# Earlier projections, earlier mask and earlier weight loads in a chain of attention, gated experts and channel mix

## The chip, the cores and the metric

One Trainium2 chip, one core. The metric is the device time of one execution in microseconds. The kernel before took 582.27 us, the median of three runs (582.23 to 583.47).

## What is computed

Three layers in a chain, float32, for 4 batches of 8 heads, 512 local and 32 global positions, width 64 a head.

```
s_ll = where(|i - j| <= 32, scale * q_l k_l^T, -1e9)      # local rows: window of 32 on both sides
a_l  = softmax([scale * q_l k_g^T, s_ll]);  out_l = a_l @ [v_g, v_l]
out_g = softmax(scale * q_g [k_g, k_l]^T) @ [v_g, v_l]    # global rows: all keys
x = concat(out_g, out_l), heads side by side              # (4, 576, 512): 544 computed tokens, 512 wide

logits = x @ w_gate; the two best of 4 experts, softmax of their logits as w
for each expert e: a = softmax(causal(scale * (x wq[e]) (x wk[e])^T)); y_e = a (x wv[e]) wo[e]
x = sum over the two chosen experts of w_e * y_e

xk = mu_k * x + (1 - mu_k) * x_prev;  xr = mu_r * x + (1 - mu_r) * x_prev     # x_prev: the token before
out = sigmoid(xr @ w_r) * (relu(xk @ w_k)^2 @ w_v)
```

## The kernel before

**Local attention, steps 0 to 35.** A loop `for n in range(NU + 4)` with NU = 32 holds the first layer as a pipeline written out by hand: step n forms the scores of two heads and half the sequence (`a_qk`, tile S, 16 matmuls), adds the mask and takes the row minimum on VectorE (`band`, tile sm, mn), and takes the exponential on ScalarE. `a_norm(n-1)` divides by the sum (rc on VectorE, pn and glob on GpSimd), `a_tp(n-2)` transposes (pT on TensorE, copied to `pts` by ScalarE or VectorE in turn). Four steps make a unit u; once a unit come the scores of the global rows (`g_qk`, Sga, pg), their weighting (`g_norm`) and transposes (`g_tp`), and `a_pv`, the product with V (tiles x, xg), which is written to `xT[b]`. Two units are one batch, so batch 0 is complete after unit 1, in step 10 or so.

**Second layer.** `b_split(b, half)` rounds a half of batch b's tokens into a high part (VectorE, L343) and a low part (GpSimd, L344), tile x00 for batch 0, half 0, then x01, x10 and on. `b_groups(b)` makes fifteen closures a batch, the splits and the projections: `b_qk` (tiles pb00q0 and on, 12 matmuls each, results in tile qk) and `b_v` (pv00 and on). A product of two float32 values is three matmuls on high and low parts (lines 93, 94, 95). The projections of batch 0 are called in steps B0 = 26 to 33 of the loop; `c_step` then runs nine causal-attention units a batch (scores C, row minima csm, transposes cT, product y) from step CS = 34 on, with the projections of the next batch between them; `last_rows` and the units named `l` do the 32 last rows (Ll, Lg, and the gate gb, gl).

**Weights and constants.** `load_wb(step)` fetches the weights of Q, K or V (rawwq, rawwk, rawwv), and `split_wb(step, c)` rounds one of their four chunks with a ScalarE cast (L154) and a GpSimd subtraction (L155). The load stands at step WB + 4 step (4, 8, 12), and one chunk is rounded in each of the four steps from there. The mask `band` is the last of four DMAs that ScalarE's queue issues at the start. At step 10 the loop fetches constants, `mu` among them, and computes `omu = 1 - mu` on VectorE.

**What sets the order.** The program is written as above, and a scheduler puts each engine's instructions in order when the kernel is built; on the chip each engine then works through its list in that order. An instruction that waits holds up all that stand behind it on its engine. Tiles come from pools: tag "x" holds one tile, and raw weights and the split tokens share it, so rawwk waits for the last subtraction of wq, x00 for the last subtraction of wv, x01 for the last matmul that reads x00. PSUM tag "a" holds six banks, taken in turn by S, Sga, pT, xg and the projections. The SP queue issues its DMAs in order, and each waits for the DMA eight places before it.

**Third layer.** From about 400 us to the end the channel mix; nothing of it is in the change.

Of the kernel before, what the change touches and what calls it, by code (L numbers as in the profile page):

```python
# [28 lines left out]
NU_D = 256  # L29
MIX, K0, FIRST = 32, 33, 4  # L30
V0, VS = 31, 2
WB, WS = 4, 4
LPOS, LPOS0 = 3, 3
B0, CS = 26, 34
BIG = 3.0e38
EPS = 1e-9
SCALE = 0.125
# [8 lines left out]
def chain_kernel(ctx: ExitStack, tc: tile.TileContext, kq, vw, vgd, w_gate, wq, wk, wv, wo,  # L46
# [12 lines left out]
    def T(tag, shape, name, dt=F32, bufs=None):  # L59
        return sb.tile([128] + list(shape), dt, tag=tag, bufs=bufs or BUFS[tag], name=name)  # L60
# [107 lines left out]
    for i in range(2):  # L168
        nc.gpsimd.memset(ptg[i][:, 4, :], 0.0)

    def load_pair(P, parts=1):
        t = T("kp", [NQ], f"kq{P}")
        if parts == 1:
            nc.sync.dma_start(t, kq[P])
        else:
            for eng, a, b in ((nc.sync, KT0, KT0 + 480), (nc.scalar, 0, 256), (nc.sync, KT0 + 480, NQ),
                              (nc.scalar, 256, 512)):
                eng.dma_start(t[:, a:b], kq[P][:, a:b])
        kqs[P] = t

    def load_v(P):
        t = T(("raw", "y", "wo")[P // 2 % 3], [2 * NB, 2 * HD], f"vw{P}")
        nc.sync.dma_start(t, vw[P].rearrange("p (j c) -> p j c", c=2 * HD))
        vws[P] = t
# [51 lines left out]
    def a_tp(n):  # L236
        u, r = divmod(n, 4)
        if r == 0:
            pts[u] = T("qk", [4, 4, 128], f"pt{u}")
        t = pn.pop(n)  # L240
        pT = ps_t(f"pT{n}")
        for k in range(4):
            nc.tensor.transpose(pT[:, k * 128:(k + 1) * 128], t[:, k].rearrange("p a b -> p (a b)"), ident)  # L243
        dst = pts[u][:, r].rearrange("p a b -> p (a b)")
        if r % 2 == 0:
            nc.scalar.copy(dst, pT)
        else:
            nc.vector.tensor_copy(dst, pT)
# [50 lines left out]
    def a_pv(u):  # L299
        b, g = divmod(u, 2)  # L300
        pt, pgt, tg = pts.pop(u), ptg[u % 2], tgs.pop(u)
        gp = ps_t(f"xg{u}")
        xs = [ps_x(f"x{u}{pp}") for pp in range(2)]
        for pp in range(2):
            v = vws.pop(2 * u + pp)
            for blk in range(2 * NB):
                m, c = divmod(blk, 2)
                for h in range(2):
                    rr = slice(64 * h, 64 * h + 64)
                    w = v[:, blk, rr]  # L310
                    nc.tensor.matmul(xs[pp][rr, 64 * blk:64 * blk + 64], w,  # L311
                                     pt[:, 2 * pp + m // 2, 2 * h + m % 2, 64 * c:64 * c + 64],
                                     start=blk == 0, stop=False, skip_group_check=True)
                    ch = m if c == 0 else (NB if m == NB - 1 else None)
                    if ch is not None:
                        hq = 32 * (2 * pp + h)
                        nc.tensor.matmul(gp[rr, 32 * pp:32 * pp + 32], w, pgt[:, ch, hq:hq + 32],
                                         start=pp == 0 and ch == 0, stop=pp == 1 and ch == NB, skip_group_check=True)
        for pp in range(2):
            rr = slice(64 * pp, 64 * pp + 64)  # L320
            nc.tensor.matmul(xs[pp], vgb[rr, u], tg[rr, :], start=False, stop=True, skip_group_check=True)
        for pp in range(2):
            p = 2 * g + pp
            nc.scalar.copy(xT[b][:, p, 1 + SG:1 + S], xs[pp])
        nc.vector.tensor_copy(xT[b][:, 2 * g:2 * g + 2, 1:1 + SG], gp[:, 0:64].rearrange("p (a c) -> p a c", a=2))
# [371 lines left out]
        g = tokens[n][0] + 128 * i  # L697
        nc.sync.dma_start(out_f[g:g + 128, :], o)

    load_pair(0, 4)  # L700
    nc.scalar.dma_start(ident, c_ident)
    nc.scalar.dma_start(band, c_band)
    load_pair(1)
    load_v(0)
    load_v(1)
    nc.sync.dma_start(vgb, vgd.rearrange("p (u c) -> p u c", u=NG))
    load_pair(2)
    load_pair(3)
    units = []
    for b in range(B):  # L710
# [43 lines left out]
            load_wd("k", w_k, k % 4, k // 4, 512 * (k // 4))  # L754

    fill = b_groups(0)
    for n in range(NU + 4):
        if n == 10:
            nc.sync.dma_start(tail, c_tail)
            nc.sync.dma_start(bsel, c_bsel)  # L760
            nc.sync.dma_start(rsel, c_rsel)
            nc.sync.dma_start(tri, c_tri)
            nc.sync.dma_start(mu[:, 0, :], mu_k.rearrange("(c p) -> p c", p=128))
            nc.sync.dma_start(mu[:, 1, :], mu_r.rearrange("(c p) -> p c", p=128))
            nc.vector.tensor_scalar(omu, mu, -1.0, 1.0, op0=ALU.mult, op1=ALU.add)
            ql = T("ql", [2, 2, 128], "ql", F32R)
            qld = [[ql[:, p, s] for s in range(2)] for p in range(2)]
            nc.gpsimd.memset(v32(ql), 0.0)
# [22 lines left out]
        if n >= WB and n < WB + 3 * WS:  # L791
            step, c = divmod(n - WB, WS)
            if c == 0:
                load_wb(step)
            if c < NC:
                split_wb(step, c)
        if B0 <= n < CS:
            k = -(-len(fill) // (CS - n))
            for g in fill[:k]:
                g()  # L800
            del fill[:k]
# [116 lines left out]
```

## Time and profile before

| | |
|---|---|
| median of three runs | 582.27 us (582.23 to 583.47) |
| the profiled execution | 579.51 us |
| its span, first to last instruction | 577.7 us |
| mean granted TensorE clock over the span | 0.982 |
| TensorE busy | 546.5 us, 95% |
| VectorE, ScalarE, GpSimd busy | 350.3, 330.8, 315.0 us |

The profiled execution took 579.51 us, 2.76 us under the median of the runs; 1.8 us of it lie around the span. TensorE is busy for 95% of the span, an average: there are stretches in which it waits for others, and a few in which the clock granted to it is lower. Where the clock is given as a share, 1.0 is 2.4 GHz and 0.5 is 1.2 GHz; a value between them is a mean over a stretch with both.

### The profile page before, as it was taken

Reading aid. Unit: us, or ns where it says so; the run is one execution under the profiler, and the core shown is the slowest. Engines: PE = TensorE matmul, PEld = TensorE weight load, DVE = VectorE, ACT = ScalarE, POOL = GpSimd, SP = SyncE. Lnnn points to the kernel's source line nnn. Section 1 sums busy time; section 2 is a strip of 40 time slices with the busy share of each in tenths; the row PEclk is TensorE's granted clock in tenths of the full one; section 3 lists DMA queues with packets and bytes.
Section 4 is the critical chain, followed back from the end, with each engine's and each line's share of the span. In section 5 each row is a group of like instructions: output and inputs, shape, how many; then the busy total and the mean of one; then the engine's idle time right before and its main releaser. Section 6 shows DMA issues by size and latency. Waiting matters only on the chain.

```text
span 577.7 us, 12767 instructions
## 1 busy us (share of the span) xinstructions
PE 546.5 (95%) x4670; PEld 456.8 (79%) x4670; DVE 350.3 (61%) x1145; ACT 330.8 (57%) x995; POOL 315.0 (55%) x416
## 2 busy tenths in 40 slices
PE   3879999999999999799899898999999999999997
PEld 2657767889987888588778786888898989898896
DVE  2545677468678668648788989969343343324211
ACT  3676777555546465347579667677444554434221
POOL 1755765465356546636567999967444444334120
PEclk9897999999999999799999999999999999999999
DMA  8974645023101101011111222010000000000000
GB/s 346 324 210 135 199 172 174 2 76 83 48 1 38 38 21 54 2 37 38 37 38 38 74 74 75 35 39 36 1 38 1 37 1 36 19 19 37 2 19 36
DMA packets 19775, 38.85 MB, mean 67 GB/s; under 512 B 9472, under 2 KB 10496, under 8 KB 19712
## 3 DMA queue, kind: packets, MB, share of 16 engines
q1 hardware_dynamic: 19136, 37.46, 19.9%
q8 instruction: 37, 0.61, 0.4%
q10 hardware_dynamic: 576, 0.57, 0.3%
q14 instruction: 26, 0.21, 0.1%
HBM read 33.57 MB, written 4.46 MB: 66 GB/s over the span
## 4 chain that ended last, share of the span: by engine, by line
PE 65%; DVE 13%; ACT 8%; POOL 5%; DMA 5%; issue 3%; SPq 1%; ACTq 0%; DVEq 0%; POOLq 0%
PE v L93 4%; PE v L94 4%; PE v L95 4%; PE k L94 4%; PE k L93 4%; PE k L95 4%; PE y L557 4%; PE cT L487 3%; PE C L101 3%; PE x L311 3%; PE r L93 2%; DVE x L343 2%; PE r L94 2%; PE r L95 2%; PE S L198 2%
## 5 line engine op out<-in xcount | busy, mean ns | idle before, releaser
L651 POOL TENSOR_TENSOR kk<-k2r,kk 128x256 fp32r<-128x256 f32 x64 | 50.6, 793 | 68.3 <-ACT kk L650 68.3
L648 DVE TENSOR_TENSOR k2r<-ksr 128x256 f32<-128x256 f32 x64 | 36.9, 578 | 70.5 <-ACT ksr L647 64.3
L479 POOL TENSOR_TENSOR csm<-csm,crc 128x128 f32<-128x128 f32 (+3 forms) x64 | 50.1, 803 | 47.3 <-DVE crc L476 22.6
L211 ACT ACTIVATE sm<-sm,mn 128x160 f32<-128x160 f32 x128 | 53.4, 419 | 23.4 <-DVE mn L208 23.1
L631 DVE SCALAR_TENSOR_TENSOR mmr<-xT,mu,mtr 128x256 f32<-128x256 f32 (+4 forms) x96 | 58.8, 648 | 10.7 <-POOL m L635 4.1
L228 POOL TENSOR_TENSOR pn<-sm,rc 128x256 f32<-128x256 f32 x64 | 38.0, 614 | 43.6 <-DVE rc L224 23.2
L463 ACT ACTIVATE csm<-csm,cmn 128x128 f32<-128x128 f32 (+3 forms) x64 | 35.8, 561 | 27.3 <-DVE cmn L461 27.3
L647 ACT ACTIVATE ksr<-k 128x256 f32<-128x256 f32 x64 | 24.1, 377 | 40.5 <-PE k L95 40.0
L630 ACT ACTIVATE mtr<-xT,omu 128x256 f32<-128x256 f32 (+4 forms) x96 | 40.3, 442 | 7.7 <-DVE mmr L631 7.0
L208 DVE CUSTOM_DVE_ANT_0 sm<-S,band 128x160 f32<-128x160 f32 x128 | 34.2, 320 | 16.9 <-DMA band<-in_band_dram 9.0
L635 POOL TENSOR_TENSOR m1L<-mmr,m1H 128x256 fp32r<-128x256 f32 (+1 forms) x36 | 27.6, 779 | 30.5 <-ACT m1H L634 30.4
L650 ACT CAST kk<-k2r 128x256 fp32r<-128x256 f32 x64 | 25.9, 404 | 25.7 <-DVE k2r L648 22.7
L198 PE MATMUL S<-kq 64*64 64x160 f32 x512 | 31.1, 325 | 7.6 <-DMA kq<-in_kq_dram 4.1
L557 PE MATMUL y<-cpt,vC 128*64 128x128 f32 (+1 forms) x320 | 35.8, 300 | 0.0
L461 DVE CUSTOM_DVE_ANT_0 csm<-C,causal 128x128 f32<-128x128 f32 (+3 forms) x64 | 29.7, 485 | 4.9 <-PE C L101 3.5
L696 DVE TENSOR_TENSOR o<-v,rt 128x512 f32<-128x512 f32 x17 | 11.6, 685 | 33.4 <-ACT m1H L634 18.2
L487 PE MATMUL cT<-ident,csm 128*128 128x128 f32 x160 | 27.0, 286 | 5.0 <-DVE cpt L492 2.4
L198 PEld LDWEIGHTS S<-kq 64*64 64x64 f32 x512 | 19.7, 140 | 15.1 <-issue 6.9
L311 PE MATMUL x<-pt,vw 128*64 128x64 f32 x512 | 30.6, 244 | 0.1
L243 PE MATMUL pT<-ident,pn 128*128 128x128 f32 x128 | 22.3, 300 | 8.1 <-DVE mng L274 4.0
L311 PEld LDWEIGHTS x<-pt,vw 128*64 128x64 f32 x512 | 25.9, 149 | 5.0 <-issue 3.9
L557 PEld LDWEIGHTS y<-cpt,vC 128*64 128x64 f32 x320 | 21.7, 137 | 9.1 <-issue 5.7
(408 smaller groups left out, 1894.7 us busy)
## 6 DMA issues: line engine op xcount, KB each, us to landing
kq<-in_kq_dram SPq DMA_DIRECT2D x15, 688.0 KB, 5.5
vw<-in_vw_dram SPq DMA_DIRECT2D x16, 512.0 KB, 4.7
out_dram<-o SPq DMA_DIRECT2D x17, 256.0 KB, 2.0
wrawk<-in_moe_w_k_dram SPq DMA_DIRECT2D x8, 512.0 KB, 3.7
wrawv<-in_moe_w_v_dram SPq DMA_DIRECT2D x8, 512.0 KB, 3.6
wrawr<-in_moe_w_r_dram SPq DMA_DIRECT2D x4, 512.0 KB, 4.0
vgb<-in_vgd_dram SPq DMA_DIRECT2D x1, 512.0 KB, 6.9
rawwq<-in_moe_wq_dram SPq DMA_DIRECT2D x4, 128.0 KB, 8.6
```

Of the source, the lines that this page charges most:

```text
L93: nc.tensor.matmul(o, wH, xH, start=start, stop=False)
L94: nc.tensor.matmul(o, wH, xL, start=False, stop=False)
L95: nc.tensor.matmul(o, wL, xH, start=False, stop=stop)
L198: nc.tensor.matmul(st[h][64 * c:64 * c + 64, i * W:(i + 1) * W], t[rr, 64 * blk:64 * blk + 64], t[rr, KT0 + 96 * blk:KT0 + 96 * blk + W], ...
L211: last_act = nc.scalar.activation(ts[:, h, i], ts[:, h, i], AF.Exp, bias=mn[:, c:c + 1], scale=-1.0, accum_out=su[:, c:c + 1])
L311: nc.tensor.matmul(xs[pp][rr, 64 * blk:64 * blk + 64], w, pt[:, 2 * pp + m // 2, 2 * h + m % 2, 64 * c:64 * c + 64], start=blk == 0, stop= ...
L479: nc.gpsimd.tensor_tensor(t[:, :w], t[:, :w], rc[:, e:e + 1].to_broadcast([128, w]), op=ALU.mult)
L487: nc.tensor.transpose(pT[:, j * 128:(j + 1) * 128], ts[e][:, j * 128:(j + 1) * 128], ident)
L557: nc.tensor.matmul(yp[64 * e:64 * e + 64, o0:o0 + n], vC[b][:, j, hh * HD:(hh + 1) * HD], pt[:, e, j, 0:n], start=j == 0, stop=j == i and ...
L630: nc.scalar.mul(mt[:, cc], xp, omu[:, kind, c:c + 1])
L631: nc.vector.scalar_tensor_tensor(mm[:, cc], x, mu[:, kind, c:c + 1], mt[:, cc], op0=ALU.mult, op1=ALU.add)
L651: nc.gpsimd.tensor_sub(hl[1], k2, v32(hl[0]))
```

## The change

It does five things.

- **Mask.** `load_pair(0, True)` puts the first two of the three parts of `band` second on the SP queue, behind 448 columns of the first keys; the third part is fourth on ScalarE's queue, behind `ident`. `load_pair(2)` moves ahead of `vgb`.
- **Weights.** They are loaded in steps 3, 7 and 11, and their four chunks rounded two a step in the third and fourth step from the load (5 and 6, 9 and 10, 13 and 14).
- **Constants.** Their DMAs are issued at step 5; `omu` and the tile `ql` are written at step 14 in the program.
- **Projections of batch 0.** The fifteen closures are called one a step from 15 to 31, none in 15 and 23; `c_step` starts at 32.
- **Tiles.** The transposed weights of units with even number lie in two tiles of tag "cpt" in place of one of tag "qk", which batch 0's projections now take earlier.

```diff
--- before.py
+++ after.py
@@ -29,9 +29,9 @@
 NU_D = 256
 MIX, K0, FIRST = 32, 33, 4
 V0, VS = 31, 2
-WB, WS = 4, 4
+WB, WS, WL = 3, 4, 2
 LPOS, LPOS0 = 3, 3
-B0, CS = 26, 34
+B0, CS = 15, 32
 BIG = 3.0e38
 EPS = 1e-9
 SCALE = 0.125
@@ -168,14 +168,18 @@
     for i in range(2):
         nc.gpsimd.memset(ptg[i][:, 4, :], 0.0)
 
-    def load_pair(P, parts=1):
+    def load_pair(P, first=False):
         t = T("kp", [NQ], f"kq{P}")
-        if parts == 1:
+        if not first:
             nc.sync.dma_start(t, kq[P])
         else:
-            for eng, a, b in ((nc.sync, KT0, KT0 + 480), (nc.scalar, 0, 256), (nc.sync, KT0 + 480, NQ),
-                              (nc.scalar, 256, 512)):
-                eng.dma_start(t[:, a:b], kq[P][:, a:b])
+            nc.sync.dma_start(t[:, KT0:KT0 + 448], kq[P][:, KT0:KT0 + 448])
+            nc.scalar.dma_start(t[:, 0:256], kq[P][:, 0:256])
+            nc.sync.dma_start(band[:, 0:2], c_band[:, 0:2])
+            nc.scalar.dma_start(t[:, 256:512], kq[P][:, 256:512])
+            nc.sync.dma_start(t[:, KT0 + 448:], kq[P][:, KT0 + 448:])
+            nc.scalar.dma_start(ident, c_ident)
+            nc.scalar.dma_start(band[:, 2:3], c_band[:, 2:3])
         kqs[P] = t
 
     def load_v(P):
@@ -236,12 +240,17 @@
     def a_tp(n):
         u, r = divmod(n, 4)
         if r == 0:
-            pts[u] = T("qk", [4, 4, 128], f"pt{u}")
+            if u % 2:
+                t = T("qk", [4, 4, 128], f"pt{u}")
+                pts[u] = [t[:, j] for j in range(4)]
+            else:
+                ts = [T("cpt", [2, 4, 128], f"pt{u}{j}") for j in range(2)]
+                pts[u] = [t[:, j] for t in ts for j in range(2)]
         t = pn.pop(n)
         pT = ps_t(f"pT{n}")
         for k in range(4):
             nc.tensor.transpose(pT[:, k * 128:(k + 1) * 128], t[:, k].rearrange("p a b -> p (a b)"), ident)
-        dst = pts[u][:, r].rearrange("p a b -> p (a b)")
+        dst = pts[u][r].rearrange("p a b -> p (a b)")
         if r % 2 == 0:
             nc.scalar.copy(dst, pT)
         else:
@@ -309,7 +318,7 @@
                     rr = slice(64 * h, 64 * h + 64)
                     w = v[:, blk, rr]
                     nc.tensor.matmul(xs[pp][rr, 64 * blk:64 * blk + 64], w,
-                                     pt[:, 2 * pp + m // 2, 2 * h + m % 2, 64 * c:64 * c + 64],
+                                     pt[2 * pp + m // 2][:, 2 * h + m % 2, 64 * c:64 * c + 64],
                                      start=blk == 0, stop=False, skip_group_check=True)
                     ch = m if c == 0 else (NB if m == NB - 1 else None)
                     if ch is not None:
@@ -697,14 +706,12 @@
         g = tokens[n][0] + 128 * i
         nc.sync.dma_start(out_f[g:g + 128, :], o)
 
-    load_pair(0, 4)
-    nc.scalar.dma_start(ident, c_ident)
-    nc.scalar.dma_start(band, c_band)
+    load_pair(0, True)
     load_pair(1)
     load_v(0)
     load_v(1)
+    load_pair(2)
     nc.sync.dma_start(vgb, vgd.rearrange("p (u c) -> p u c", u=NG))
-    load_pair(2)
     load_pair(3)
     units = []
     for b in range(B):
@@ -754,14 +761,16 @@
             load_wd("k", w_k, k % 4, k // 4, 512 * (k // 4))
 
     fill = b_groups(0)
+    NFILL = len(fill)
     for n in range(NU + 4):
-        if n == 10:
+        if n == 5:
             nc.sync.dma_start(tail, c_tail)
             nc.sync.dma_start(bsel, c_bsel)
             nc.sync.dma_start(rsel, c_rsel)
             nc.sync.dma_start(tri, c_tri)
             nc.sync.dma_start(mu[:, 0, :], mu_k.rearrange("(c p) -> p c", p=128))
             nc.sync.dma_start(mu[:, 1, :], mu_r.rearrange("(c p) -> p c", p=128))
+        if n == 14:
             nc.vector.tensor_scalar(omu, mu, -1.0, 1.0, op0=ALU.mult, op1=ALU.add)
             ql = T("ql", [2, 2, 128], "ql", F32R)
             qld = [[ql[:, p, s] for s in range(2)] for p in range(2)]
@@ -792,10 +801,11 @@
             step, c = divmod(n - WB, WS)
             if c == 0:
                 load_wb(step)
-            if c < NC:
-                split_wb(step, c)
+            if c >= WL:
+                split_wb(step, 2 * (c - WL))
+                split_wb(step, 2 * (c - WL) + 1)
         if B0 <= n < CS:
-            k = -(-len(fill) // (CS - n))
+            k = NFILL * (n + 1 - B0) // (CS - B0) - NFILL * (n - B0) // (CS - B0)
             for g in fill[:k]:
                 g()
             del fill[:k]
```

From 171 us of the run before on (the transposes of the causal unit 002), each engine's order is the same in both. Before that point the instructions move. Three places show it. Names are the program's, with the step, unit or batch in them.

ScalarE, around the exponentials of step 9 (sm9) and the cast of the weights of K (wk). Before:

```order
L246 COPY pt1_408<-pT6_554 128x512
L154 CAST wk_560<-rawwk_561 128x256
L211 ACTIVATE sm9_578,su9_580<-sm9_578,mn9_579 128x160 x4
L154 CAST wk_560<-rawwk_561 128x256
L277 ACTIVATE pg0_90,sug2_600<-pg0_90,mng2_599 128x544
```

With the change:

```order
L215 ACTIVATE sm8_550,su8_552<-sm8_550,mn8_551 128x160 x4
L255 COPY pt1_416<-pT6_568 128x512
L215 ACTIVATE sm9_584,su9_586<-sm9_584,mn9_585 128x160 x4
L154 CAST wk_534<-rawwk_535 128x256 x2
L286 ACTIVATE pg0_90,sug2_606<-pg0_90,mng2_605 128x544
L215 ACTIVATE sm10_650,su10_652<-sm10_650,mn10_651 128x160 x3
L255 COPY pt20_672<-pT8_674 128x512
L215 ACTIVATE sm10_650,su10_652<-sm10_650,mn10_651 128x160
L154 CAST wk_534<-rawwk_535 128x256 x2
```

The first cast of wk stood ahead of sm9; now both stand behind it, and the casts go two by two.

VectorE, around the casts that round batch 0's first half of tokens (x00). Before they stood behind the row minima of step 16:

```order
L223 TENSOR_SCALAR rc15_1069<-su15_1011 128x4
L224 RECIPROCAL rc15_1069<-rc15_1069 128x4
L208 ISA sm16_1058,mn16_1059<-S16_1_1049,band_68 128x160
L208 ISA mn16_1059 128x1
L208 ISA sm16_1058,mn16_1059<-S16_1_1049,band_68 128x160
L208 ISA mn16_1059 128x1
L343 CAST x00_1727<-xT0_81 128x256 x4
L208 ISA sm17_1092,mn17_1093<-S17_0_1082,band_68 128x160
L208 ISA mn17_1093 128x1
L208 ISA sm17_1092,mn17_1093<-S17_1_1083,band_68 128x160
```

With the change, from the end of step 14's minima on (rc14 is the reciprocal of its sum):

```order
L212 ISA sm14_911,mn14_912<-S14_1_902,band_68 128x160
L212 ISA mn14_912 128x1
L227 TENSOR_SCALAR rc14_1025<-su14_913 128x4
L228 RECIPROCAL rc14_1025<-rc14_1025 128x4
L352 CAST x00_1085<-xT0_81 128x256 x4
L334 COPY xT1_83<-xg2_940 128x2x32
L212 ISA sm15_1014,mn15_1015<-S15_0_1004,band_68 128x160
L212 ISA mn15_1015 128x1
L212 ISA sm15_1014,mn15_1015<-S15_0_1004,band_68 128x160
L212 ISA mn15_1015 128x1
```

The four casts moved from behind step 16 to between steps 14 and 15, and ahead of the copy of xg2 into xT1. They still wait for the last GpSimd subtraction of wv, whose four subtractions now stand before, between and behind the weighting of steps 13 and 14 on GpSimd, the last one behind pn14 and glob3.

VectorE, around the gate of the last rows (gatel, gb), which TensorE reads in the matmul gl. Before, gb is ready eleven rows ahead of the casts of batch 1's second half (x11):

```order
L431 TENSOR_TENSOR gb_2418<-gatel_2416,bsel_70 128x16
L474 TENSOR_SCALAR crc002_2555<-csu002_2477 128x2
L475 RECIPROCAL crc002_2555<-crc002_2555 128x2
L364 TENSOR_TENSOR qk10_2350<-pb10k0_2498,qk10_2350 128x256
L476 TENSOR_TENSOR crc002_2555<-crc002_2555,gate0_2165 128x2
L492 COPY cpt000_2528<-cT0001_2532 128x128
L509 ISA pl_2369,lmn0_2549<-Ll0_2535,zcol_73 128x272
L509 ISA lmn0_2549 128x1
L511 ISA pl_2369,lmn0_2549<-Lg0_2536,tail_69 128x272
L511 ISA lmn0_2549 128x1
L513 TENSOR_TENSOR lmn0_2549<-lmn0_2549 128x1
L343 CAST x11_2576<-xT1_83 128x288 x4
```

With the change; the last cast of x11 stands three rows above the first row here:

```order
L416 TENSOR_REDUCE gsl_2528<-gdl_2524 128x1
L470 ISA csm0030_2614,cmn003_2604<-C0030_2606,causal_2253 128x512
L470 ISA cmn003_2604 128x1
L532 RECIPROCAL lrc0_2625<-lrc0_2625 128x1
L417 TENSOR_SCALAR gsl_2528<-gsl_2528 128x1
L470 ISA csm0031_2617,cmn003_2604<-C0031_2607,causal_2253 128x512
L470 ISA cmn003_2604 128x1
L418 RECIPROCAL gsl_2528<-gsl_2528 128x1
L373 TENSOR_TENSOR qk11_2283<-pb11q0_2463,qk11_2283 128x256
L373 TENSOR_TENSOR qk11_2283<-pb11k0_2562,qk11_2283 128x256
L420 TENSOR_TENSOR gatel_2532<-gdl_2524,gsl_2528 128x4
L440 TENSOR_TENSOR gb_2534<-gatel_2532,bsel_70 128x16
```

The gate moved from ahead of the casts to behind them, behind the minima of unit 003 and the low parts of qk11. On TensorE the matmul gl stands ahead of the projections pv12 and pv13 in both.

## Rows read from the trace of the kernel before

**Rows 1.** The page's first part: each engine's busy us, its share of the span, and its instructions.

```profile
PE 546.5 (95%) x4670; PEld 456.8 (79%) x4670; DVE 350.3 (61%) x1145; ACT 330.8 (57%) x995; POOL 315.0 (55%) x416
```

**Rows 2.** Stretches of the run side by side: the stretch in us and its length, then the busy us of PE, PEld, DVE, ACT and POOL with the number of instructions, the mean granted TensorE clock as a share of full speed, the mean share of the DMA engines in use, GB/s.

```profile
75.00:160.00 85.00, 84.93 (x1138) 69.93 (x1136) 57.25 (x284) 53.94 (x187) 44.03 (x70) 1.00 0.27 86
...
40.00:44.20 4.20, 0.15 (x6) 0.03 (x1) 0.92 (x7) 2.35 (x10) 1.30 (x2) 0.90 0.61 183
44.20:51.40 7.20, 7.20 (x102) 6.08 (x102) 3.18 (x17) 3.37 (x12) 5.00 (x9) 0.59 0.26 76
10.00:20.00 10.00, 6.41 (x63) 4.72 (x67) 7.21 (x49) 8.12 (x36) 5.67 (x11) 0.66 1.08 371
230.00:240.00 10.00, 6.36 (x42) 4.47 (x40) 7.51 (x24) 3.99 (x14) 5.31 (x8) 0.72 0.04 16
```

**Rows 3.** The chain of waits that ended last, its longest pieces in order of time: start, length, and what the chain spent it on.

```profile
2.12 7.77 DMA band<-in_band_dram
...
14.41 7.21 DMA vw<-in_vw_dram
...
21.64 4.73 DMA mu<-in_moe_mu_r_dram
...
38.31 2.78 DMA rawwk<-in_moe_wk_dram
...
57.73 3.87 DMA rawwv<-in_moe_w_gate_dram
```

**Rows 4.** VectorE in order of time at the start, around step 5 and around step 9: start, length, the instruction, and in brackets the idle time before it with what ended it.

```profile
10.04 0.33 DVE L208 CUSTOM_DVE_ANT_0 sm<-S,band 128x160 f32<-128x160 f32 x1 [9.04 <-DMA band<-in_band_dram]
...
26.46 0.17 DVE L765 TENSOR_SCALAR omu<-mu 128x8 f32<-128x8 f32 x1 [1.48 <-DMA mu<-in_moe_mu_r_dram]
26.54 0.69 DVE L274 CUSTOM_DVE_ANT_0 pg<-Sga,zcol 128x512 f32<-128x512 f32 x1
...
43.28 0.17 DVE L223 TENSOR_SCALAR rc<-su 128x4 f32<-128x4 f32 x1 [4.04 <-ACT sm L211]
```

**Rows 5.** ScalarE in order of time at the weights of K (41 us) and V (61 us): the casts, and the exponential of the global scores behind the second of them.

```profile
41.19 0.40 ACT L154 CAST wk<-rawwk 128x256 fp32r<-128x256 f32 x1 [2.91 <-DMA rawwk<-in_moe_wk_dram]
...
61.70 0.72 ACT L154 CAST wv<-rawwv 128x260 fp32r<-128x260 f32 x2 [2.08 <-DMA rawwv<-in_moe_w_gate_dram]
62.32 0.74 ACT L277 ACTIVATE pg<-pg,mng 128x544 f32<-128x544 f32 x1
```

**Rows 6.** TensorE in order of time: the transposes of step 8 behind its longest wait, and steps 15 to 18.

```profile
44.20 1.09 PE L243 MATMUL pT<-ident,pn 128*128 128x128 f32 x4 [4.04 <-DVE mng L274]
...
66.23 0.66 PE L293 MATMUL pTG<-ident,pg 128*128 128x128 f32 x4 [0.38 <-POOL pg L286]
...
66.92 0.76 PE L198 MATMUL S<-kq 64*64 64x160 f32 x8
...
73.85 1.01 PE L198 MATMUL S<-kq 64*64 64x160 f32 x16 [0.97 <-DVE mn L208]
```

**Rows 7.** VectorE in order of time in steps 14 to 17: the row minima of step 14 (63.32) and step 15 (66.44), the evacuation of xg, and the casts that round batch 0's first half of tokens (L343).

```profile
63.20 0.15 DVE L284 TENSOR_SCALAR rcg<-sug 128x1 f32<-128x1 f32 x1 [2.67 <-ACT pg L277]
63.32 0.32 DVE L208 CUSTOM_DVE_ANT_0 sm<-S,band 128x160 f32<-128x160 f32 x1
...
66.33 0.19 DVE L325 COPY xT<-xg 128x64 f32<-128x64 f32 x1
66.44 0.32 DVE L208 CUSTOM_DVE_ANT_0 sm<-S,band 128x160 f32<-128x160 f32 x1
...
70.52 2.45 DVE L343 CAST x<-xT 128x256 fp32r<-128x256 f32 x4 [0.27 <-POOL wv L155]
```

**Rows 8.** GpSimd in the same stretch: a low part of the weights of V (L155) and the weighting of step 14 (L228, L231).

```profile
66.13 0.75 POOL L155 TENSOR_TENSOR wv<-rawwv,wv 128x260 fp32r<-128x260 f32 x1
66.83 1.19 POOL L228 TENSOR_TENSOR pn<-sm,rc 128x256 f32<-128x256 f32 x2
67.97 0.41 POOL L231 TENSOR_TENSOR glob<-sm,rc 128x128 f32<-128x128 f32 x1
```

**Rows 9.** TensorE in order of time behind batch 1's projection pb11k: transposes, the gate's matmul gl, the first of pv12, and products y.

```profile
158.82 0.60 PE L487 MATMUL cT<-ident,csm 128*128 128x128 f32 x4
...
160.62 0.40 PE L438 MATMUL gl<-gb,rsel 128*128 128x16 f32 x2
...
161.60 0.39 PE L93 MATMUL pv<-wv,x 128*128 128x260 f32 x1 [0.22 <-DVE cpt L492]
...
162.40 0.65 PE L557 MATMUL y<-cpt,vC 128*64 128x128 f32 x6
```

**Rows 10.** VectorE in the same stretch: the casts of batch 1's second half of tokens, the copy of cT001, the row minima of the causal unit 003 and the low parts of qk11.

```profile
159.09 2.07 DVE L343 CAST x<-xT 128x288 fp32r<-128x288 f32 x4 [0.85 <-PE pb11k L95]
...
161.14 0.41 DVE L492 COPY cpt<-cT 128x256 f32<-128x256 f32 x1
...
161.54 0.67 DVE L461 CUSTOM_DVE_ANT_0 csm<-C,causal 128x512 f32<-128x512 f32 x1
...
162.84 0.41 DVE L364 TENSOR_TENSOR qk<-pb11q,qk 128x256 fp32r<-128x256 f32 x1
```

**Rows 11.** TensorE around 235 us, where a half of batch 2's tokens gives way to the next.

```profile
233.80 0.36 PE L93 MATMUL pv<-wv,x 128*128 128x260 f32 x1 [1.77 <-DVE x L343]
...
236.55 0.66 PE L487 MATMUL cT<-ident,csm 128*128 128x128 f32 x2 [1.88 <-DVE cpt L492]
```


## The prediction

> **What bounds the kernel now.** I read the page's engine totals first: TensorE is busy for 95% of the span, the next engine for 61% [rows 1]. That is an average, so I read the stretches next. From 75 to 160 us TensorE is busy 84.93 of 85 us at full clock [rows 2]; there, where the projections of batch 0 stand now, only less TensorE work would help, and the change has as much as before. What it can take away lies ahead of 75 us, and what it can break is the cover behind. The chain of waits names the early stops: 7.77 us for the mask, 4.73 us for mu behind 7.21 us of vw DMAs, 2.78 us for the weights of K, 3.87 us for those of V [rows 3]. The orders of both programs agree from 171 us on, so what is won or lost before that is carried to the end one for one; I take no gain or loss behind it.
>
> **What it takes away.**
>
> The start. The first row minimum waits 9.04 us for the mask [rows 4]. Two thirds of the mask now come second on SP, but step 1 needs the third part, which is still fourth on ScalarE's queue, where the last DMA took 7.77 us [rows 3]. Then `omu` holds VectorE: it waits 1.48 us for mu, and the minimum of the global scores stands behind it [rows 4]. The order still has omu there, now between steps 4 and 5, though the program writes it at step 14. Mu's DMAs go ahead of vw4 and vw5; the wait should go, and no more, since step 5 cannot pass omu. I take 1.5 us; bounds 0 (mu as late as now) and 3.
>
> Weights of K. ScalarE waits 2.91 us for rawwk and casts 0.40 [rows 5], with the exponentials of step 9 behind it; VectorE waits 4.04 us for those, TensorE 4.04 us for VectorE [rows 4, 6]. Now the exponentials stand ahead of the cast, and the load is ahead of vw7 and kq7 on SP: 2.91 + 0.40 = 3.3, and a little of the GpSimd work behind it, 3.4 us. Bounds 2.9 and 4.04.
>
> The clock behind that wait. TensorE is busy 0.15 us of the 4.20 up to 44.20, and over the next 7.20 us the granted clock is 0.59 [rows 2], so 0.82 of them, 5.9 us, run at 1.2 GHz. Four transposes take 1.09 us there and 0.66 at full clock [rows 6], 0.39 less. 5.9 x 0.39 = 2.3 us; bounds 0 (it falls for another reason) and 2.95 (half of all).
>
> Sum: 1.5 + 3.4 + 2.3 = 7.2 us.
>
> **What it adds.** No arithmetic is added; four places lose their cover.
>
> x00. The four casts now stand between the minima of steps 14 and 15 on VectorE, and wait for the last subtraction of wv. The chain from the first minimum of step 14: the reciprocal done, 66.33 - 63.32 = 3.0 us [rows 7]; a copy of pt now between the exponentials, 0.6; then on GpSimd pn 1.19, glob 0.41 and the last subtraction 0.75 [rows 8], 2.35; some 0.25 for the subtraction ahead of pn; the casts 2.45 and the copy of xg 0.19 [rows 7]. In all 8.8 us, against 3.1 from step 14 to step 15 now. The scores of step 16 need the bank which that copy frees. Where does TensorE stand then? Step 14 was late, since VectorE waited for pg, and pg for the cast of wv, which waited 2.08 us for its DMA [rows 5, 7]. The load is earlier now, so step 14 starts at 63.32 - 2.08 = 61.2 (in times of the run before), the bank is free at 70.0, and TensorE is there at 66.92 - 0.38 = 66.5 [rows 6]: a stop of 3.5 us. The present casts' wait of 0.97 and the 0.38 go [rows 6], which leaves 2.2; steps 15 and 16, with VectorE, ScalarE and GpSimd in turn, cost some 0.8 more. I take 3.0; bounds 0 (covered) and 5 (the DMA of wv as late as now).
>
> The clock behind that stop. It is nearly as long as the 4.04 that was followed by 2.3 us of loss. What follows waits for other engines too, so I take half, 1.2; bounds 0 and 2.3.
>
> x01. Its casts wait for the last matmul on x00 (pb00's and pb01's, pb01k0 last), and the minima of step 23 stand behind them: about 2.45 + 0.41 (a low part, as for qk11) + two minima at 0.32 = 3.5 us [rows 7, 10]. TensorE has scores 0.76, transposes 0.66 twice, and some short products [rows 6], 2.5 us. I take 1.0; bounds 0 and 2.
>
> x10. The products of unit 7 that stood behind the last projection of batch 0 now stand partly ahead of it. Casts of 2.07 us and a low part of 0.41 [rows 10] come ahead of the minima of unit 000; TensorE's transposes and short products cover about half. I take 1.0; bounds 0 and 2.5.
>
> gl. TensorE reads the gate gb in gl, ahead of pv12 and pv13. Now gb stands behind the casts of x11 (159.09 to 161.1), a copy (0.41), two minima (161.54 to 162.8) and two low parts of 0.33 each, with two short operations of its own: 163.9 [rows 10]. TensorE comes to gl at 160.62 [rows 9], plus the products y now ahead of it, 0.65 and a little: 161.5. It waits 2.4, and the 0.22 ahead of pv goes [rows 9]: 2.2; bounds 0 and 3.3 (no y left to cover it).
>
> Sum: 3.0 + 1.2 + 1.0 + 1.0 + 2.2 = 8.4 us. The two copies into "cpt" tiles are as long as the one into "qk", and the DMAs of the constants pass vw4 and vw5, which are wanted a unit later: nothing for either; without that slack they would stop unit 2's products, by up to the 7.21 us these DMAs take in the chain [rows 3].
>
> **The numbers.** 8.4 - 7.2 = +1.2 us: 579.51 + 1.2 = 580.7 for an execution like the profiled one, which lay 2.76 under the median of 582.27. I give the time against the median: **583.5 us**. A measurement of this kernel can tell 0.2%, 1.16 us, from no change: the forecast lies just on the slower side of 583.4.
>
> **A rule to weigh.** After 4.04 us of idling the clock was 0.59 [rows 2, 6]. The 10 us from 230 have 0.72, with stops of 1.77 and 1.88 and little work between them [rows 2, 11]; the start, 10 to 20 us, with TensorE busy 6.41 of 10, has 0.66 [rows 2]. The Trainium skill says in "TensorE: Matmul & The Clock Gate", section "HAM oscillation", that a long enough wait puts the array back to 1.2 GHz, so the work behind each such wait starts cold, every time. The trace agrees; by that rule both long stops here would cost their 2.3 in full, the second rival.
>
> **Rivals.**
> - *The stops are covered.* TensorE is the bound at 95%, and there may be more of its work ahead of each stop than I count. For it: no idle from 75 to 160 us. Against it: the x tile is single, so its casts can't start early. If all four are covered: 582.27 - 7.2 - (0.97 + 0.38 + 0.22) = 573.5, chance 0.10. If x00's alone is: 582.27 - 7.2 - 1.35 + 1.0 + 1.0 + 2.2 = 577.9, **faster**, chance 0.21. It decides whether TensorE reaches step 16's scores later than the copy of xg2.
> - *Each stop also halves the clock.* x00 in full, 2.3 for 1.2, and 2.3 behind gl: 583.5 + 3.4 = 586.9; with the DMA of wv still late, 2 more, 588.9. Chance 0.19.
> - *The weights of K don't come earlier*, so the change does not do what it says: SP waits for the last subtraction of wq all the same, and the 4.04 stay, with their clock: 583.5 + 3.4 + 2.3 = 589.2. Against it: the exponentials stand ahead of the cast. Chance 0.07.
> - The forecast, 580.5 to 587 by the bounds of its small terms: 0.43.
>
> Faster by over 0.2% (under 581.1): 0.10 + 0.21 + 0.04 of the forecast's range = 0.35. Within: 0.17, from the forecast's range. Slower: 0.22 + 0.19 + 0.07 = 0.48. Range 576.5 to 589.5: it leaves out the fully covered case and little else.
>
> **What would show it.** Right: TensorE's idle of 4.04 at 40 us gone, with full clock behind it; omu without a wait; a stop of 3 to 4 us ahead of step 16's scores, with VectorE in the casts of x00 or waiting for GpSimd's subtraction of wv; one of about 2 us ahead of gl, ended by gb. Wrong: no stop ahead of step 16, or a second row of clock near 0.6 behind gl, or a new wait for a DMA (vw5, kq9) between 40 and 75 us. From gl to the end the two traces should differ by a constant.

## The result and the profile after

The changed kernel takes **590.24 us** (median of six runs, 587.85 to 592.51) against 581.88 of six runs of the kernel before beside it: ratio 1.0142, 95% interval 1.0104 to 1.018, some 8.4 us **slower**. The forecast had the side right and the size wrong: 583.5, with 589.5 as the upper end. The median lies between three runs of 587.85 to 588.55 us, the profiled one among them, and three of 591.93 to 592.51, whose mean granted clock is lower (0.967 to 0.968 against 0.976 to 0.982). The profiled execution took 588.16 us, its span 586.4 against 577.7, so 8.7 us more.

The engine totals of the page hardly differ from [rows 1]:

```profile
PE 548.5 (94%) x4670; PEld 457.1 (78%) x4670; DVE 346.9 (59%) x1145; ACT 331.6 (57%) x995; POOL 314.7 (54%) x416
```

The stretches of after (columns as in [rows 2]) show where time is lost. TensorE, busy for all but 0.07 us from 75 to 160 us before, idles there for 2.5 us, and three stretches of low clock stand where none was. The low clock behind the weights of K is gone (0.59 before, 1.00 in the third row here), and so is that of the start: 0.66 over 10 to 20 us before, 1.00 over the same 10 us now.

```profile
75.00:160.00 85.00, 82.46 (x1122) 66.64 (x1121) 50.05 (x260) 51.87 (x182) 41.04 (x66) 0.98 0.28 88
...
26.00:34.00 8.00, 7.11 (x114) 6.12 (x114) 4.52 (x27) 6.04 (x23) 4.64 (x7) 0.57 0.75 274
...
44.00:52.00 8.00, 7.27 (x141) 5.72 (x143) 5.46 (x30) 6.40 (x24) 6.62 (x11) 1.00 0.39 132
...
68.00:74.00 6.00, 5.52 (x52) 3.06 (x56) 4.13 (x25) 4.45 (x18) 3.02 (x6) 0.72 0.12 45
140.00:146.00 6.00, 4.29 (x20) 3.90 (x21) 5.19 (x21) 3.97 (x14) 3.19 (x5) 0.72 0.44 131
170.00:176.00 6.00, 5.13 (x43) 4.92 (x44) 3.77 (x19) 1.82 (x5) 3.09 (x3) 1.00 0.00 0
```

TensorE in order of time names the stops, with the idle time in brackets. Two of them, at 26.31 and 141.72, were in no term of the forecast:

```profile
26.31 1.03 PE L202 MATMUL S<-kq 64*64 64x160 f32 x6 [4.47 <-DVE mn L212]
...
44.73 0.63 PE L252 MATMUL pT<-ident,pn 128*128 128x128 f32 x4 [1.15 <-DVE mng L283]
...
68.48 0.76 PE L202 MATMUL S<-kq 64*64 64x160 f32 x8 [2.83 <-DVE xT L334]
...
141.72 0.37 PE L93 MATMUL pb01k<-x,wk 128*128 128x288 f32 x1 [2.20 <-DVE mn L212]
...
168.31 0.65 PE L566 MATMUL y<-cpt,vC 128*64 128x128 f32 x6 [0.58 <-DVE lrc L531]
...
170.87 0.37 PE L447 MATMUL gl<-gb,rsel 128*128 128x16 f32 x2 [1.91 <-DVE crc L483]
```

The chain of waits of after, to hold against [rows 3]: the mask lands 1.6 us sooner (8.31 against 9.89), mu at 25.34 against 26.37, the weights of K and V are gone from it, and a load of the third layer has come in:

```profile
2.12 6.19 DMA band<-in_band_dram
...
21.61 3.73 DMA mu<-in_moe_mu_r_dram
...
134.24 4.95 DMA wrawk<-in_moe_w_k_dram
```

VectorE at the places of [rows 4, 7], and once more at 140 us. `omu` waits 4.62 us where it waited 1.48, and now the minima of step 5 stand behind it; rc, which waited 4.04 us at step 9, waits 1.15; the x00 casts stand idle for 2.92 us first; a low part of pb01q waits 5.50 for ScalarE.

```profile
25.44 0.17 DVE L774 TENSOR_SCALAR omu<-mu 128x8 f32<-128x8 f32 x1 [4.62 <-DMA mu<-in_moe_mu_r_dram]
25.59 0.33 DVE L212 CUSTOM_DVE_ANT_0 sm<-S,band 128x160 f32<-128x160 f32 x1
...
43.81 0.17 DVE L227 TENSOR_SCALAR rc<-su 128x4 f32<-128x4 f32 x1 [1.15 <-ACT sm L215]
...
66.41 1.89 DVE L352 CAST x<-xT 128x256 fp32r<-128x256 f32 x4 [2.92 <-DMA vw<-in_vw_dram]
...
140.20 0.46 DVE L373 TENSOR_TENSOR qk<-pb01q,qk 128x288 fp32r<-128x288 f32 x1 [5.50 <-ACT qk L372]
```

The profile puts the x00 wait down to a load of vw, which in the chain of waits lands at 66.42. GpSimd's last subtraction of wv ends at 66.37, so this trace can't tell the two apart; in the kernels of the experiments omu later, woH later and projections back, which have the casts at the same place, the profile names the subtraction for the same wait (2.92, 2.93 and 2.92 us):

```profile
65.64 0.73 POOL L155 TENSOR_TENSOR wv<-rawwv,wv 128x260 fp32r<-128x260 f32 x1
```

The SP queue shows why mu is late: the four DMAs of rawwq hold the queue for 6.51 us (5.83 before), tail and bsel for 4.3 more (1.6 before), and mu's second DMA is issued at 21.61. Before it was issued at 21.64, though two loads of vw (3.07 us) stood ahead of it there: passing them won 0.03 us.

```profile
8.53 6.51 SPq L143 DMA_DIRECT2D rawwq<-in_moe_wq_dram  x4
15.09 2.59 SPq L767 DMA_DIRECT2D tail<-in_tail_dram  x1
17.72 1.69 SPq L768 DMA_DIRECT2D bsel<-in_bsel_dram  x1
...
21.61 0.51 SPq L772 DMA_DIRECT2D mu<-in_moe_mu_r_dram  x1
```

and before:

```profile
21.64 0.38 SPq L764 DMA_DIRECT2D mu<-in_moe_mu_r_dram  x1
```

ScalarE at 43 us and at 136 to 140 us. The casts of wk no longer wait. But woH and wyk, the first roundings of the output weights and of the third layer's, stand ahead of the evacuation of pb01q, and each waits for a DMA that starts only when unit 6 gives its V buffers back (its products with V run from 131.9 to 134.1 us, the two DMAs are issued at 132.69 and 134.24):

```profile
43.69 0.69 ACT L154 CAST wk<-rawwk 128x256 fp32r<-128x256 f32 x2
...
136.40 1.05 ACT L340 CAST woH<-rawwo 128x1024 fp32r<-128x1024 f32 x1 [2.22 <-DMA rawwo<-in_moe_wo_dram]
...
139.21 0.67 ACT L126 ACTIVATE wyk<-wrawk 128x512 f32<-128x512 f32 x1 [0.79 <-DMA wrawk<-in_moe_w_k_dram]
139.79 0.38 ACT L372 CAST qk<-pb01q 128x288 fp32r<-128x288 f32 x1
```

### The profile page after: what moved, and what is told of

Read it like the earlier page. It is cut to its first block, busy times and chain, and to the rows that moved or that the text cites. A ratio compares the mean times of both kernels' runs of the same rounds, so it can differ in the third digit from the quotient of the medians.

```text
span 586.4 us, 12771 instructions
## 1 busy us (share of the span) xinstructions
PE 548.5 (94%) x4670; PEld 457.1 (78%) x4670; DVE 346.9 (59%) x1145; ACT 331.6 (57%) x995; POOL 314.7 (54%) x416
## 4 chain that ended last, share of the span: by engine, by line
PE 67%; DVE 13%; ACT 8%; POOL 5%; issue 3%; DMA 3%; SPq 0%; ACTq 0%; DVEq 0%; POOLq 0%
PE v L93 4%; PE v L94 4%; PE v L95 4%; PE k L94 4%; PE k L93 4%; PE k L95 4%; PE y L566 4%; PE S L202 3%; PE x L320 3%; PE C L101 3%; PE cT L496 3%; PE pT L252 2%; ACT sm L215 2%; PE r L93 2%; PE r L94 2%
## 5 line engine op out<-in xcount | busy, mean ns | idle before, releaser
L202 PE MATMUL S<-kq 64*64 64x160 f32 x512 | 33.2, 331 | 12.6 <-DVE mn L212 4.8
L101 PE MATMUL C<-qk 64*128 64x128 f32 (+3 forms) x192 | 27.7, 362 | 0.3 <-DVE lg L389 0.3
```

Of the source, the lines that this page charges most:

```text
L101: nc.tensor.matmul(op[0], op[a], op[x], start=n == 0, stop=n == 2)
L202: nc.tensor.matmul(st[h][64 * c:64 * c + 64, i * W:(i + 1) * W], t[rr, 64 * blk:64 * blk + 64], t[rr, KT0 + 96 * blk:KT0 + 96 * blk + W], ...
```

## The experiments

All start from the changed kernel. A time is the median of its runs; a ratio is against the kernel before on the same chip, with its 95% interval. The chips differ a little (the kernel before took 581.18 to 582.37 us on them), so a difference of two times is good to about 1 us. `issue_after(x)` places an instruction behind x on its own engine; `last_min` is the newest of the row minima, `last_act` the newest exponential.

**omu later.**

```diff
+            with tc.issue_after(last_min.ins):        # minima of step 13
                 nc.vector.tensor_scalar(omu, mu, -1.0, 1.0, ...)
```

> The changed kernel with one edit: omu is held behind the row minima of step 13 on VectorE (it stands ahead of step 5 in the change). Theory A (omu waits 4.62 us for mu ahead of step 5, TensorE stops 4.47 us and then runs near half clock until 33 us): that stop and the clock behind it go, unit 0's last product (34.11 us) comes at 27 to 30 us, and the time falls from 590.2 by 4 to 7.3 us to 583 to 586; a DMA that is now too slow may keep up to 3 of it. Theory B (the spread projections cost it all): the time stays within 2 us of 590, since what is won at the start is lost again at later waits.

584.2 us, ratio 1.0043 (1.0015 to 1.0072), 6.0 below the changed kernel. The stop of 4.47 us is gone and with it the low clock, and unit 0's last product starts at 27.79 instead of 34.11 us (30.68 in the kernel before); in place of 0.57 the stretch now reads:

```profile
24.00:34.00 10.00, 9.69 (x175) 7.36 (x179) 6.76 (x41) 7.70 (x28) 7.75 (x13) 1.00 0.89 321
```

**x00 later.**

```diff
+            with tc.issue_after(last_min.ins) if (b, half) == (0, 0) else ExitStack():   # minima of step 16
                 nc.vector.tensor_copy(hl[0][:, c, :n], x)
```

> The changed kernel with one edit: the casts of x00 are held behind the row minima of step 16, as before. Theory A: the stop of 2.83 us ahead of step 16's scores goes, with 1.5 us of lowered clock behind it, and a wait of about 1 us comes back at step 18: 586.5 to 588. Theory B (TensorE makes it up later, the projections being delayed instead): 589.5 to 591.

585.78 us, ratio 1.0105 (1.0052 to 1.0157), 4.4 below the changed kernel by the medians. One of the five runs took 591.70, and the interval overlaps that of the changed kernel (1.0104 to 1.018): alone this gain isn't clear of the noise. With omu it is, as the run of both shows. No stop stands at step 16; the first projection waits 0.98 us instead:

```profile
71.77 0.36 PE L93 MATMUL pv<-wv,x 128*128 128x260 f32 x1 [0.98 <-DVE mn L212]
```

**woH later.** A miss.

```diff
+        with tc.issue_after(last_act.ins):            # exponentials of step 31
             nc.scalar.copy(woS[0], raw)
```

> The changed kernel with one edit: the cast of the output weights (woH) is held behind the exponentials of step 31 on ScalarE. Theory A (the cast waits 2.2 us for its DMA ahead of the cast of pb01q, VectorE waits 5.5 us for that one with step 31's minima behind it, TensorE stops 2.2 us ahead of pb01k and runs at half clock for some 4 us): both go, 3.5 to 4.1 us, 586 to 587. Theory B (another wait takes its place, or the stop is given back at gl): within 1.5 us of 590.

595.52 us, ratio 1.0233 (1.0177 to 1.029): slower still by the median, though the two intervals touch. ScalarE's wait passed from woH to wyk, and the stop stayed:

```profile
141.03 0.66 ACT L126 ACTIVATE wyk<-wrawk 128x512 f32<-128x512 f32 x1 [3.01 <-DMA wrawk<-in_moe_w_k_dram]
```

```profile
143.53 0.58 PE L93 MATMUL pb01k<-x,wk 128*128 128x288 f32 x1 [2.37 <-DVE mn L212]
```

So two transfers stand ahead of the evacuation, and taking woH's away alone is worth nothing (wyk's alone was not tried). Why it is 5 us slower on top was not tested; its profiled execution, 597.14 us, has granted clocks of 0.96 and 0.53 in the two stretches of 10 us from 240 us, far from the edit, where the changed kernel has 0.83 and 1.00.

**Projections back in steps 26 to 33** (`B0, CS = 26, 34`).

> The changed kernel with B0, CS back at 26, 34, all else as changed (mask, weights, constants, tiles); x00 stays between the minima of steps 14 and 15, omu ahead of step 5. Theory A: the stops ahead of pb01k and gl go (2.2 and 2.5 us and 2 of clock), the start's loss of 3.4 and the stop at x00 stay: 583 to 585. Theory C (spreading is harmless, start and x00 are the whole loss): 589 to 591. Theory B (spreading is the whole loss): 576 to 578.

585.48 us, ratio 1.0076 (1.0051 to 1.01), 4.8 below the changed kernel and half a us above theory A's range. The stops at pb01k and gl are gone. That at omu stays (5.18), and so does that of x00 (3.12): the scheduler puts the x00 casts early whether or not a projection asks for them, probably because the weights are rounded early (not tested by itself).

**omu and x00 later**, both edits above.

> Both single edits together: omu behind step 13's minima and the four x00 casts behind step 16's minima. Theory A (each stop costs its own time, in its own place): the gains of the two alone, 6.0 and 4.4 us, add up: 590.2 - 10.4 = 579.8 us, 579 to 582, with the stops at step 5's scores (4.47) and step 16's scores (2.83) both gone and those at pb01k (2.2) and gl (2.5) left. Theory B (PE has a fixed amount of work that other engines feed it, and a stop taken out early comes back further on): 583 to 585, about what either alone gives.

579.0 us, ratio 0.9952 (0.9924 to 0.998): the two gains, 10.4 us in sum, gave 11.2. The interval lies clear of that of omu alone, so x00's stop has its price too, and the stops in different places add up.

**The same with the projections in steps 26 to 33.**

> omu behind step 13's minima and x00 behind step 16's, with the projections back in steps 26 to 33 (B0 26, CS 34): what is left of the change are the mask, the early weights and the buffers of pt. If the gains add up: 585.5 - 6.0 - 4.4 = 575.1 us, 574 to 577, below the kernel with the same two edits and spread projections (579.8 expected) by about 4.7. If spreading is worth something once its stops are gone (theory of the change: fillers cover PE's waits in the local attention), this one is no faster than the kernel in which the weights and the gate are moved too (573.5 to 575.5 expected). If x00 behind step 16 matters less where no projection asks for it: 579 to 580.

Here `last_min` is of step 26 when x00 is asked for, so its casts stand behind step 26's minima (97.51 us), not step 16's as the expectation says.

574.75 us, ratio 0.9868 (0.9839 to 0.9898). Every gain added up here too, and without the spread projections the kernel is 4.25 us faster than with them.

**All third-layer roundings held back**, on top of the two edits. A miss. woH is asked for at causal step 6, so that it stands behind the sixth step's exponentials (the expectation says the eighth's), and in `load_wd`

```diff
+        with tc.issue_after(last_act.ins):            # now also the causal steps' exponentials
             nc.scalar.activation(v32(g), hf, AF.Sign, bias=tcol)
             nc.scalar.activation(v32(y), hf, AF.Abs)
```

> On top of the two edits the output weight's rounding woH stands behind the scaling exponentials of the eighth causal step, and the third-layer weights' first activations (wyk) behind those of the step in which they are asked for, so that no evacuation on ScalarE stands behind a transfer. Theory A (the stop of 2.2 us at pb01k and the low clock behind it come from ScalarE waiting for the two transfers rawwo and wrawk): the stop at pb01k is gone, 576 to 577.5 us, about 3 below the kernel with the two edits. Theory B (DVE is what is late there, by its casts of x10 and the split of qk): the stop stays at 1.5 to 2.5 us, time within 1 us of the kernel with the two edits.

581.3 us, ratio 0.9985 (0.9958 to 1.0012). The stop at pb01k went, and yet it is 2.3 us slower than with the two edits: the edit also held back the later weights of the third layer, which TensorE then waits for behind 340 us, for instance for wr0H, where the kernel before waited 0.43:

```profile
356.88 1.22 PE L93 MATMUL r<-wr0H,m1H 128*128 128x512 f32 x2 [2.57 <-ACT wr0H L133]
```

The next kernel, which has the gate one step earlier on top, has the same stretch and misses its range as well:

> On top of that, the last rows' gate one step earlier (at n = NU + 2), which puts gatel and gb ahead of the four x11 casts on DVE. Theory A (the stop of 2.5 us at gl is the gate's chain standing behind the x11 casts): stop gone, 2 to 3 us below the kernel without this edit, 573.5 to 575.5 us. Theory B (the gate's chain is only moved, and the scores or the pv product ahead of it wait in its place): 0 to 1 us below.

580.85 us, ratio 0.9983 (0.9957 to 1.0008). In its trace the stretch at 342 us is half idle and at half clock, and a stop of 1.97 stands ahead of the last rows' product in place of that at gl:

```profile
342.00:350.00 8.00, 4.52 (x10) 2.45 (x11) 7.34 (x10) 4.46 (x12) 8.00 (x9) 0.58 0.29 113
350.00:358.00 8.00, 4.50 (x9) 2.05 (x8) 6.97 (x10) 5.96 (x15) 7.86 (x7) 0.50 0.29 90
```

```profile
147.48 0.39 PE L93 MATMUL pvl<-wv,xlH 128*128 128x260 f32 x1 [1.97 <-DVE xlH L435]
```

**Only the first of the third-layer weights held back**, with woH still at causal step 6 and the two edits.

```diff
+        with tc.issue_after(last_act.ins) if (name, c, k) == ("k", 0, 0) else ExitStack():
```

> The two edits (omu, x00), woH late, and of the third-layer weights the first (wyk00) alone held behind a causal step's exponentials; all other activations of such weights where the change has them. If the 9 us of stops and the 18 us at half clock behind 340 us came from the later weights' activations being held as well (theory A), they are gone, and the stop at pb01k stays gone: 575 to 577 us, 2 to 4 below the kernel with the two edits (579.0). If they come from the attention ending earlier than the weights can follow, or from woH (theory B), they stay: 580 to 582.

576.12 us, ratio 0.9902 (0.988 to 0.9924), 2.9 below the two edits. No stop at pb01k, and the stretch at 340 is as in the kernel before: with both transfers away from the evacuation the stop goes, with woH's alone (above) it stays. With the gate one step earlier:

> On top of that the last rows' gate at n = NU + 2. With the stop at gl gone and one of up to 2 us at pvl in its place (as seen in the kernel with all weights held), 574 to 577 us, 0 to 2 below the kernel without it. Against 574.75 for the projections in steps 26 to 33 with the same omu and x00: if spreading is worth something once all its stops are out, this is at 572 or below; if the spread projections only move PE's work about, 574 to 577.

577.22 us, ratio 0.9923 (0.9898 to 0.9947): no gain. The stop only moved, from gl to the last rows' product (1.97 again).

**x11 behind the gate.** `tc.issue_after(last_gb.ins)` around the x11 casts, with the gate in its own step:

> Spread projections, omu and x00 late, woH and wyk00 late (the kernel at 576.12), and the four x11 casts behind gb on DVE, so that the last rows' gate doesn't stand behind them, while gate and pvl stay in their step. Theory A (the stop of 1.85 us at gl and the 1.7 us of low clock behind it are x11's): both gone, 572.5 us, 571.5 to 574. Theory B (the stop goes elsewhere: the scores' second minimum, or the last query's scale, stands behind the casts): 575 to 577. At 572.5 spreading would be worth some 2 us against 574.75 for the projections in steps 26 to 33; at 575 or more it is worth nothing even with its stops taken out one by one.

574.24 us, ratio 0.9871 (0.9847 to 0.9895), 1.9 below; expected were 572.5. The stop at gl falls from 1.85 to 0.48:

```profile
155.41 0.37 PE L451 MATMUL gl<-gb,rsel 128*128 128x16 f32 x2 [0.48 <-DVE gb L444]
```

This is the spread version with these stops out. It is as fast as the one with the projections in steps 26 to 33 (574.75, ratio 0.9868), which has none of the three edits to woH, the first weight and x11: spreading itself is worth nothing that could be measured here. The idle time that it was to fill was there: with the projections in steps 26 to 33 TensorE stops for 1.15 us once a unit up to 95 us, and with the spread ones the three stops behind 66 us are gone. Yet at the end of pb20q, at 217.4 us, the two traces are level. From 28 us to there TensorE idles some 1.8 us less with the spread projections and is busy some 1.8 us longer, at full clock in both; why it is busy longer was not tested.

**Weights as before**, in the kernel at 574.75. A miss in size.

```diff
-WB, WS, WL = 3, 4, 2
+WB, WS, WL = 4, 4, 0
```

(and `split_wb` once a step; nothing else is changed)

> omu and x00 late, projections in steps 26 to 33 (as in the kernel at 574.75), and the weights of Q, K, V loaded and rounded as before the change (WB 4, one block a step). If the wait for wk and the low clock behind it are what the early weights are worth (theory A: 5.6 us), 580 to 581; if they are worth nothing when the local attention's stops are gone (theory B), 574.5 to 575.5. What is left below 581.5 is the mask behind the first keys and the buffers of pt: 0.5 to 1.5.

585.13 us, ratio 1.0058 (1.0036 to 1.0079): the early weights are worth 10.4 us, not 5.6. From unit 0's last product to unit 1's it takes 19.36 us, and on to unit 2's 18.19, where both take 14.10 with the early weights: 5.3 for K, near the 5.6 expected, and 4.1 for V.

```profile
28.32 1.13 PE L330 MATMUL x<-tg,vgb 64*128 64x512 f32 x4
...
47.68 1.13 PE L330 MATMUL x<-tg,vgb 64*128 64x512 f32 x4
...
65.87 1.13 PE L330 MATMUL x<-tg,vgb 64*128 64x512 f32 x4
```

TensorE stops twice, once for rawwk as in the kernel before, and once more for rawwv, which there cost it little ([rows 5, 6]: 2.08 on ScalarE, 0.38 on TensorE):

```profile
41.87 1.09 PE L252 MATMUL pT<-ident,pn 128*128 128x128 f32 x4 [4.08 <-DVE mng L283]
...
60.99 1.09 PE L252 MATMUL pT<-ident,pn 128*128 128x128 f32 x4 [3.85 <-DVE mng L283]
```

```profile
38.85 0.40 ACT L154 CAST wk<-rawwk 128x256 fp32r<-128x256 f32 x1 [2.93 <-DMA rawwk<-in_moe_wk_dram]
...
57.98 0.41 ACT L154 CAST wv<-rawwv 128x260 fp32r<-128x260 f32 x1 [2.70 <-DMA rawwv<-in_moe_w_gate_dram]
```

## Why the prediction was wrong

Place for place, in the two profiled executions (positive is lost). Clock losses are estimates: a stretch times one minus its granted clock.

| Term | Forecast | Measured | How |
|---|---|---|---|
| start | -1.5 | **+3.4** | unit 0's last product starts at 34.11 against 30.68 |
| weights of K, with clock | -5.7 | -5.6 | from there to unit 1's, 14.10 against 19.68 |
| x00, with clock | +4.2 | +3.2 | 2.83 - 0.97 - 0.38 + 6.00 x 0.28 |
| x01 and x10 | +2.0 | 0 | no stop there |
| pb01k, with clock | none | **+3.9** | 2.20 + 6.00 x 0.28 |
| gl | +2.2 | +2.3 | 0.58 + 1.91 - 0.22 |
| sum | +1.2 | +7.2 | |

The marks of the first two lines and of pb10k, on TensorE in order of time, after and then before:

```profile
34.11 0.70 PE L330 MATMUL x<-tg,vgb 64*128 64x512 f32 x2
...
48.21 0.70 PE L330 MATMUL x<-tg,vgb 64*128 64x512 f32 x2
...
178.97 0.40 PE L93 MATMUL pb10k<-x,wk 128*128 128x288 f32 x1
```

```profile
30.68 0.70 PE L321 MATMUL x<-tg,vgb 64*128 64x512 f32 x2
...
50.36 0.70 PE L321 MATMUL x<-tg,vgb 64*128 64x512 f32 x2
...
171.28 0.40 PE L93 MATMUL pb10k<-x,wk 128*128 128x288 f32 x1
```

By the second half of pb10k the changed kernel is 7.7 us behind (178.97 against 171.28 for its first matmul), and 1.0 us of the 8.7 follows later; 0.5 of the 7.7 has no line in the table. From pb10k on the two orders agree, and the forecast took no difference there; a stop of 1.62 us at 294.69, which was 1.46 before, is now followed by low clock (0.72 over 294 to 300 us).

**The step that failed is the start:** "Mu's DMAs go ahead of vw4 and vw5; the wait should go, and no more". I took omu's present wait off, but a wait is the difference of two times, and the change moved both. VectorE came to omu at 25.44 - 4.62 = 20.8 us instead of 25.0: the reciprocal of step 4 was done 3.15 us sooner, since the first row minimum, which needs only the first part of the mask, ran at 5.26 instead of 10.04, and the four minima of step 5, 1.0 us, no longer stood ahead of omu. Mu landed only 1.0 us earlier, since its last DMA was issued no earlier than before (21.61 against 21.64). And omu had passed the minima of step 5, which I had read from the order ("step 5 cannot pass omu") and priced at nothing. My bounds, 0 to 3 of gain, held no loss. The experiment on omu alone shows the price: 6.0 us, with the low clock that followed the stop. It also shows what the start wins without that stop: unit 0's last product starts 2.9 us ahead of the kernel before (27.79 against 30.68), near my upper bound.

**A term was missing: pb01k.** I listed who waits for the spread projections' inputs (x00, x01, x10), and not what their evacuations stand behind. In the kernel before, woH waited 0.73 us there and wyk not at all, and the next evacuation came 5 us behind; now pb01q's stands right behind both. The experiments settle that these transfers are the cause: with woH's away the stop stays (2.37), with both away it is gone, whether the later weights are held back too or not.

**What held.** The weights of K with their clock, to 0.1 us, which is partly luck: the stop fell from 4.04 to 1.15, 2.9 us where 3.4 was forecast, and that leaves 2.7 for the clock where 2.3 was. K's size held also with the start mended (5.3 in the last experiment); what the forecast did not see is that V's loads, which cost TensorE 0.38 in the kernel before, cost 4.1 there. The mechanism of x00, its place and the stop, 2.83 for 3.5. And gl, 2.5 us of waiting for 2.4. For x01 and x10, TensorE's own work covered the casts.

**The rivals.** "The stops are covered" fell, and so did "the weights of K don't come earlier". "Each stop also halves the clock" holds in part, though it had 2.3 us of clock at x00, where 1.7 was lost, and 2.3 at gl, where none was, and its 586.9 was short for the same reasons as the forecast: the granted clock was 0.57 behind the stop of 4.47, 0.72 in the stretches around those of 2.83 and 2.20, but 1.00 behind the 1.91 at gl. The Trainium skill ("TensorE: Matmul & The Clock Gate", section "HAM oscillation") has the array cold behind every long enough wait. The trace agrees for these three stops. Behind the one of 1.91 it stayed at 2.4 GHz, and so it did behind 2.16 us at pb01k in the kernel at 579.0 (1.00 from 133 to 139 us), while behind 1.85 us at gl in the kernel at 576.12 it did not:

```profile
157.00:163.00 6.00, 5.37 (x32) 5.32 (x32) 2.44 (x11) 1.24 (x5) 3.09 (x3) 0.72 0.00 0
```

**What stays open.** Why executions of the changed kernel lie up to 4.7 us apart: their mean granted clocks point to stretches of low clock, but only one of them has a trace. Why a like stop is followed by low clock in one execution and not in another. And what holding back wyk's rounding alone would do.

## What to carry to other kernels

Where a change makes a wait's consumer earlier, work out anew both times, that at which the engine arrives and that at which the data lands; the old wait is not the amount to be won, and the bound must reach below zero. When work is moved into a stretch that had none of it, read for each engine that evacuates it what stands ahead in its queue, above all instructions that wait for a DMA. Idle time that is filled is not yet time won: here the spread projections took away three stops of 1.15 us, and both placements still gave the same time.

## What the runs showed of the hardware

The clock did not fall in the same way behind like waits. Two kernels with the same start, waits of 0.77 and 0.75 us at 12.6 and 14.0 us and no other of over 0.4 us between the first scores (4.0 us) and 21 us, had granted clocks of 1.00 and 0.68 there (the kernel at 576.12, then that at 574.24):

```profile
12.00:21.00 9.00, 6.93 (x73) 4.51 (x73) 5.33 (x35) 6.83 (x29) 5.01 (x9) 1.00 1.05 332
```

```profile
12.00:21.00 9.00, 7.62 (x61) 4.62 (x65) 5.27 (x35) 6.83 (x29) 5.06 (x10) 0.68 1.03 333
```

It cost the second little there: with TensorE slower, three short waits of 0.25 to 0.31 us are not there, and unit 0's last product starts at 27.58 against 27.52. At pb01k, too, a stop of 2.20 us was followed by 0.72 (the changed kernel) and one of 2.16 by 1.00 (the kernel at 579.0).
